# Fetching streamed weights two blocks at a time, with the first blocks of each group kept as one tile

**Chip, cores, metric.** One core of one Trainium2 chip. The metric is the device time of one execution in us; lower is better. Names of engines: PE (TensorE) does the matrix products, DVE (VectorE) and ACT (ScalarE) work on their results, SP (SyncE) issues the transfers of the weights from memory (DMAs).

## The reference

Two layers alternate, each twice, on 2048 tokens of width 640 in bf16: (A) attention over segments of 32 tokens with a recurrent memory of 8 tokens, 32 heads of 192; (B) a small mixer with shifts and two GELUs.

```python
for s in range(n_seg):                        # 64 segments, one after the other
    h = concatenate([mem, x[:, s*32:(s+1)*32]])          # 40 tokens
    q, k, v = h @ Wq, h @ Wk, h @ Wv          # 640 -> 32 x 192 each
    o = softmax(mask(q k^T * scale)) v        # per head
    o = o @ Wo                                # 32 x 192 -> 640
    mem, out[s] = o[:, :8], o[:, 8:]          # the memory feeds the next segment
# mixer: gelu(ln(x) @ w1), shifts, @ w2, residual, gelu(ln @ w3) @ w4, residual
```

The attention weights are 31 MB, of which the kernels below keep some 20 MB on the chip; the recurrence asks for all of them in every segment.

## The kernel before

Attention of both A layers runs together, one layer five segments behind the other, so a step is 80 columns wide. There are 69 steps of 8 head groups; each group has four kinds of weight blocks of 128 rows: k, q and v (5 blocks each) and o (6). The mixer runs in 35 chunks between the steps. A fixed set of blocks stays resident, the rest is streamed in every step, each block by one DMA from the SP queue into a ring. A planner in the kernel simulates all operations with assumed durations, including the DMA, and fixes each engine's order of instructions from that.

```python
RES_BYTES = 154700
RING_A = 10        # slots of one block, attention
RING_B = 5         # slots of one block, mixer
DMA_RATE = 325.0e3 # the planner's assumption, bytes per us
DMA_LAT = 2.2
... # in Plan.place(), for an operation with a DMA:
    srv = max(s + DMA_LAT, srv) + o.dma / DMA_RATE
    done = srv + 0.4
...
    # resident blocks are chosen by a running share: spread evenly among the streamed ones
    for u in rest:
        n = 2 * w_len(u)
        acc += share * n
        if acc >= n / 2 and n <= left:
            res_set.add(u)
            acc -= n
            left -= n
...
def load_unit(t, u, due):                     # u = (kind, group, block)
    ...                                       # resident: load once
    b = Slotted("ra", None)
    b.make = lambda: wring.tile([P, GW], bf16, name="wst", tag=f"ra{b.slot}")
    def fn(op):
        nc.sync.dma_start(out=T(b)[:, 0:n], in_=w_src(u))
    add("SP", 0.06, due, fn, w=(b,), dma=P * n * 2, queue="wa")
    return b, lambda: T(b)
...
# the last product of a step; the o blocks of the last groups may be put off to the step's end
for c in range(GC):
    due = base + STEP - 1 + 0.02 * g if g >= NG - OT_BUFS + 1 else s0 + 2.0 * sl
    wb, wv = load_unit(t, ("o", g, c), ...)
    def f8(op, wv=wv, c=c):
        for m in range(KC):
            nc.tensor.matmul(out=o[:, m, c0:c0 + N], lhsT=w[:, m * P:(m + 1) * P], rhs=o_[:, c, 0:N], ...)
    add("PE", mm_us(N, k=KC), due, f8, r=(wb, B("oT", G % OT_BUFS)), a=(psy,))
```

Of the kernel before, what the change touches and what calls it, by code (L numbers as in the profile page):

```python
# [12 lines left out]
bf16 = mybir.dt.bfloat16  # L13
# [6 lines left out]

LAG = 5
HG = 4
RES_BYTES = 154700
O_RES = 8
RING_A = 10
RING_B = 5
STEP = 48.0
PSUM_BANKS = {"y": 1, "x": 7}
PSUM_USES = {"y": ("y", 1), "P": ("x", 4), "S": ("x", 3), "B": ("x", 2)}
# [205 lines left out]
def kernel(  # L235
# [16 lines left out]
    nc = tc.nc  # L252
    P = 128
    _, S, Dm = A_x.shape
# [5 lines left out]
    KC = Dm // P  # L260
    FC = F // P
    assert (Dm, F, Dh, H, SEG, M) == (640, 1536, 192, 32, 32, 8) and S % (2 * SEG) == 0 and NSEG > 8
    NG = H // HG
    GW = HG * Dh
    GC = GW // P
# [5 lines left out]
    QD = Dm // 4  # L271
# [99 lines left out]
    def B(*key):  # L371
        if key not in bufs:
            bufs[key] = Buf()
        return bufs[key]
# [3 lines left out]
    add = plan.add  # L378
# [9 lines left out]
    def T(b):  # L388
        if b.obj is None:
            b.obj = b.make()  # L390
        return b.obj
# [8 lines left out]
        return ((172 if ps_ else 224) + n) / 1200.0 + 0.02  # L400


    ORDER = []
    for g in range(NG):
        for kind in ("k", "q", "v"):
            ORDER += [(kind, g, kc) for kc in range(KC)]
        if g:
            ORDER += [("o", g - 1, c) for c in range(GC)]
    ORDER += [("o", NG - 1, c) for c in range(GC)]

    def w_len(u):
        return Dm if u[0] == "o" else GW

    res_set = {u for u in ORDER if u[0] == "o" and u[1] >= O_RES}
    left = RES_BYTES - sum(2 * w_len(u) for u in res_set)
    rest = [u for u in ORDER if u not in res_set]
    share = left / sum(2 * w_len(u) for u in rest)
    acc = 0.0
    for u in rest:
        n = 2 * w_len(u)  # L420
        acc += share * n
        if acc >= n / 2 and n <= left:
            res_set.add(u)
            acc -= n
            left -= n

    def w_src(u):
        kind, g, c = u
        if kind == "o":
            return Wo_v[:, g, c, :]  # L430
        return W_v[kind][:, c, GW * g:GW * (g + 1)]

    resident = {}

    def load_unit(t, u, due):
        n = w_len(u)
        if u in res_set:
            if u not in resident:
                tl = wres.tile([P, n], bf16, name="w%s%d_%d" % u)
                b = Buf()  # L440

                def fn(op):
                    nc.sync.dma_start(out=tl[:], in_=w_src(u))
                add("SP", 0.06, due, fn, w=(b,), dma=P * n * 2, queue="wa")
                resident[u] = (b, lambda: tl)
            return resident[u]
        b = Slotted("ra", None)
        b.make = lambda: wring.tile([P, GW], bf16, name="wst", tag=f"ra{b.slot}")

        def fn(op):  # L450
            nc.sync.dma_start(out=T(b)[:, 0:n], in_=w_src(u))
        add("SP", 0.06, due, fn, w=(b,), dma=P * n * 2, queue="wa")
        return b, lambda: T(b)

    def load_b(nm, n, due):

        b = Slotted("rb", None)
        b.make = lambda: wring.tile([P, Dm], bf16, name="wstB", tag=f"rb{b.slot}")
        k = {"w1": n, "w3": KC + n, "w2": KC + FC}.get(nm)
        if nm == "w4":  # L460
            src = w4_v[:, n, :]
        elif nm == "w2" and n < 4:
            src = B_w2[QD * n:QD * n + P, :]
        else:
            src = wbd[k]
        rd = [] if nm == "w4" or (nm == "w2" and n < 4) else [B("wbd", k)]

        def fn(op):
            nc.sync.dma_start(out=T(b)[:], in_=src)
        add("SP", 0.06, due, fn, r=rd, w=(b,), dma=P * Dm * 2, queue="wb")  # L470
        return b, lambda: T(b)

    def order_mixer_weights():

# [35 lines left out]
    def attention_step(t):  # L510
# [12 lines left out]
        def proj_kq(g, s0):  # L523
            G = t * NG + g
            for kind, off in (("k", 0.0), ("q", 0.3 * sl)):
                pq = ps("P", [P, GC, NS], f32, "ps" + kind)
                now = []
                for kc in range(KC):
                    due = s0 + off + kc * 0.05
                    wb, wv = load_unit(t, (kind, g, kc), due)  # L530

                    def fn(op, pq=pq, wv=wv, kc=kc):
                        w, o = wv(), T(pq)
                        for c in range(GC):
                            nc.tensor.matmul(out=o[:, c, 0:N], lhsT=w[:, c * P:(c + 1) * P], rhs=h[:, kc, c0:c0 + N],  # L535
                                             start=pq.begin(), stop=True, skip_group_check=True)
                    now.append(add("PE", mm_us(N, k=GC), due, fn, r=(wb, *hk), a=(pq,), after=last[0]))
                last[0] = now
                if kind == "q":
                    q = qT[G % 2]  # L540

                    def fq(op, pq=pq, q=q):
                        nc.scalar.copy(out=q[:, :, 0:N], in_=T(pq)[:, :, 0:N])  # L543
                    add("ACT", act_us(GC * N), s0 + off, fq, r=(pq,), w=(B("qT", G % 2),))
                else:
                    k_ = kT[G % 2]

                    def fk(op, pq=pq, k_=k_):
                        p4 = T(pq)[:].rearrange("p (h c) n -> p h c n", h=2)
                        k4 = k_[:].rearrange("p (h c) n -> p h c n", h=2)  # L550
                        nc.vector.tensor_copy(out=k4[:, :, 0::3, 0:N], in_=p4[:, :, 0::2, 0:N])  # L551
                    add("DVE", dve_us(4 * N), s0 + off, fk, r=(pq,), w=(B("kT", G % 2, 0),))

                    def fk2(op, pq=pq, k_=k_):
                        p4 = T(pq)[:].rearrange("p (h c) n -> p h c n", h=2)
                        k4 = k_[:].rearrange("p (h c) n -> p h c n", h=2)
                        for hf in range(2):
                            nc.vector.tensor_tensor(out=k4[:, hf, 1:3, 0:N],
                                                    in0=p4[:, hf, 1:2, 0:N].to_broadcast([P, 2, N]),
                                                    in1=halves[:].unsqueeze(2).to_broadcast([P, 2, N]), op=ALU.mult)  # L560
                    add("DVE", 2 * dve_us(2 * N), s0 + off, fk2, r=(pq,), w=(B("kT", G % 2, 1),))

        def proj_v(g, due0):
            G = t * NG + g
            V_, vs = Vt[G % V_BUFS], vTs[G % VT_BUFS]
            vk, Vk = B("vTs", G % VT_BUFS), B("V", G % V_BUFS)
            pv = ps("P", [P, GC, NS], f32, "psv")
            now = []
            for kc in range(KC):
                due = due0 + kc * 0.05  # L570
                wb, wv = load_unit(t, ("v", g, kc), due)

                def fv(op, wv=wv, kc=kc):
                    w, o = wv(), T(pv)
                    for c in range(GC):
                        nc.tensor.matmul(out=o[:, c, 0:N], lhsT=w[:, c * P:(c + 1) * P], rhs=h[:, kc, c0:c0 + N],  # L576
                                         start=pv.begin(), stop=True, skip_group_check=True)
                now.append(add("PE", mm_us(N, k=GC), due, fv, r=(wb, *hk), a=(pv,), after=last[0]))
            last[0] = now

            def fe(op):
                nc.scalar.copy(out=vs[:, :, 0:N], in_=T(pv)[:, :, 0:N])  # L582
            add("ACT", act_us(GC * N), due0, fe, r=(pv,), w=(vk,))
            pt = ps("P", [NS, GC, P], bf16, "psvt")

            def ft(op):
                for c in range(GC):
                    nc.tensor.transpose(out=T(pt)[0:N, c, :], in_=vs[:, c, 0:N], identity=ident[:, :])  # L588
            add("PE", mm_us(P, k=GC), due0 - 2, ft, r=(vk,), w=(pt,))

            def fe2(op):
                nc.scalar.copy(out=V_[0:N, :, 0:Dh], in_=T(pt)[0:N].rearrange("n c f -> n (c f)").rearrange(  # L592
                    "n (i e) -> n i e", i=HG))
            add("ACT", act_us(GW), due0 - 2, fe2, r=(pt,), w=(Vk,))

        def attend(g):
# [65 lines left out]
            add("DVE", dve_us(GC * N), hi - 4, f7, r=(pso,), w=(B("oT", G % OT_BUFS),))  # L662
            for c in range(GC):
                due = base + STEP - 1 + 0.02 * g if g >= NG - OT_BUFS + 1 else s0 + 2.0 * sl
                wb, wv = load_unit(t, ("o", g, c), s0 + (1.9 if g < NG - 1 else 1.2) * sl + 0.03 * c)

                def f8(op, wv=wv, c=c):
                    w, o = wv(), T(psy)
# [163 lines left out]
    def chunk(c):  # L832
# [88 lines left out]
        for i, (a, e) in enumerate(((0, 3), (3, KC))):  # L921
            pz = ps("B", [P, 3, XB], f32, "psh")
            for n in range(a, e):
                due = D(0.15 + 0.04 * n)
                wb, wv = load_b("w1", n, due)

                def fw(op, n=n, a=a, wv=wv, pz=pz):
                    w, o = wv(), T(pz)
# [13 lines left out]
        hs = [ps("B", [XB, HC], f32, "hs") for _ in range(2)]  # L942
        for n in range(5):
            due = D(0.4 + 0.04 * n)
            wb, wv = load_b("w2", n, due)

            def fw(op, n=n, wv=wv):
                w = wv()
# [25 lines left out]
        for i in range(4):  # L974
            a, e = 3 * i, 3 * i + 3
            pz = ps("B", [P, 3, XB], f32, "psh2")
            for n in range(a, e):
                due = D(0.7 + 0.04 * n)
                wb, wv = load_b("w3", n, due)

                def fw(op, n=n, a=a, wv=wv, pz=pz):
                    w, o = wv(), T(pz)
# [6 lines left out]
    def chunk_end(c):  # L989
# [4 lines left out]
        y2 = [ps("B", [XB, HC], f32, "y2") for _ in range(2)]  # L994
        for n in range(FC):
            due = D(1.2 + 0.03 * n)
            wb, wv = load_b("w4", n, due)

            def fw(op, n=n, wv=wv):
                w = wv()  # L1000
# [120 lines left out]
```

## Time and profile before

| | before |
|---|---|
| time | 3761.1 us median (3757.2 to 3765.1, 4 runs) |
| PE busy, DMA engines busy | 92%, 89% |
| DMAs on the SP queue | 5,644 |
| PE's waits for a DMA, 120 to 3640 us, by start spacing | 218 us |

"By start spacing" is my own count and is used throughout: for every group of equal matmuls in the trace I take the time from its start to the next group's start, less the number of matmuls times the usual spacing of their shape (36 ns for 80 columns). The excess is put under whatever the profile names as the end of the wait. It is more than the idle time, which leaves out the pipeline running empty (a matmul of 80 columns lasts 0.20 us in the record, and the next one starts 0.036 us later). The idle time itself is in the view of waits; of the kernel before, 120 to 3640 us (total us, times, longest us):

```profile
PE psk L535 <- DMA wst<-in_A_Wk_dram: 92.5, 92, 2.9
PE psv L576 <- DMA wst<-in_A_Wv_dram: 40.0, 76, 2.1
PE psq L535 <- DMA wst<-in_A_Wq_dram: 39.4, 57, 2.0
PE psk L535 <- ACT hT L695: 19.3, 62, 0.3
PE psy L670 <- DVE oT L661: 16.8, 66, 0.8
```

PE waits mostly for streamed blocks of k, q and v (tile wst).

### The profile page before, as it was taken

The page shows a single profiled execution, that of the slowest core. Times are in us where ns is not written, and L with a number is a line of the kernel's source. Part 1 is how long each engine was busy: PE and PEld are TensorE (multiplying, and loading weights), DVE is VectorE, ACT ScalarE, POOL GpSimd, SP SyncE. Part 2 cuts the span into 40 slices and gives each one's busy share as a digit, 9 for nine tenths or more (in the row PEclk, how much of TensorE's full clock was granted, in tenths as well). Part 3 has the DMA queues.
Part 4 walks back from the last instruction along what each step waited for, and adds up shares of the span by engine and source line. Part 5 has one row for each costly group of instructions (what it writes and reads, how often), then busy time and mean ns, then how long its engine had stood idle before and what let it go on. Part 6 is the DMA issues. An engine that isn't in the chain of part 4 may idle for free.

```text
span 3769.2 us, 193200 instructions
## 1 busy us (share of the span) xinstructions
PE 3457.7 (92%) x84703; PEld 3279.4 (87%) x84703; DVE 2370.4 (63%) x6957; ACT 1727.7 (46%) x3516; POOL 306.8 (8%) x525
## 2 busy tenths in 40 slices
PE   5899999999999999999999999999999999999886
PEld 4788889898999988888999998998999999998774
DVE  1456666666666666666666666666666666666454
ACT  1344444444454544444545454444445444444332
POOL 2000000000000000000000000000000000000000
PEclk9999999999999999999999999999999999999998
DMA  9999898888898988888999988888999988889996
GB/s 316 292 301 284 281 282 272 278 282 281 279 285 271 286 272 268 269 281 277 288 284 283 288 281 276 280 276 278 283 284 288 287 276 280 274 281 288 287 293 190
DMA packets 821967, 1055.33 MB, mean 280 GB/s; under 512 B 95230, under 2 KB 817676, under 8 KB 821120
## 3 DMA queue, kind: packets, MB, share of 16 engines
q1 hardware_dynamic: 812608, 1026.89, 86.2%
q0 software_dynamic: 8512, 16.08, 1.3%
q8 instruction: 662, 10.85, 1.2%
q14 instruction: 185, 1.52, 0.1%
HBM read 1037.35 MB, written 8.19 MB: 277 GB/s over the span
## 4 chain that ended last, share of the span: by engine, by line
PE 66%; DMA 28%; issue 3%; DVE 2%; ACT 1%; SPq 0%; POOL 0%; POOLq 0%; ACTq 0%; DVEq 0%
PE psy L670 13%; PE psk L535 12%; DMA wst<-in_A_Wk_dram 11%; PE psv L576 11%; PE psq L535 10%; DMA wst<-in_A_Wv_dram 7%; DMA wst<-in_A_Wq_dram 5%; PE psvt L588 4%; PE pso L655 3%; PE pss L607 3%; PE y L1002 2%; PE psh L984 2%; PE pst L640 1%; PE hs L952 1%; PE psh L930 1%
## 5 line engine op out<-in xcount | busy, mean ns | idle before, releaser
L535 PEld LDWEIGHTS <-wst 128*128 128x128 bf16 x11592 | 529.2, 100 | 184.0 <-DMA wst<-in_A_Wk_dram 115.5
L661 DVE CAST oT<-pso 128x480 bf16<-128x480 f32 (+1 forms) x552 | 342.3, 620 | 436.6 <-PE pso L655 433.6
L535 PE MATMUL psk<-hT,wk 128*128 128x80 bf16 (+1 forms) x10764 | 590.6, 199 | 26.3 <-ACT hT L695 19.8
L670 PE MATMUL psy<-oT,wo 128*128 128x80 bf16 (+1 forms) x10005 | 574.5, 199 | 23.1 <-DVE oT L661 18.2
L592 ACT COPY V<-psvt 80x768 bf16<-80x768 bf16 (+1 forms) x552 | 438.7, 795 | 339.0 <-PE psvt L588 331.4
L535 PE MATMUL psq<-hT,wq 128*128 128x80 bf16 (+1 forms) x10764 | 554.6, 199 | 7.1 <-DMA wq<-in_A_Wq_dram 4.2
L543 ACT CAST qT<-psq 128x480 bf16<-128x480 f32 (+1 forms) x552 | 292.4, 530 | 557.9 <-PE psq L535 557.3
L576 PE MATMUL psv<-hT,wv 128*128 128x80 bf16 (+1 forms) x9936 | 526.0, 200 | 2.8 <-DMA wv<-in_A_Wv_dram 1.1
L535 PEld LDWEIGHTS <-wk 128*128 128x128 bf16 x10764 | 468.3, 100 | 38.7 <-issue 27.8
L670 PEld LDWEIGHTS <-wo 128*128 128x128 bf16 x10005 | 450.9, 100 | 45.0 <-issue 27.9
L535 PEld LDWEIGHTS <-wq 128*128 128x128 bf16 x10764 | 450.4, 99 | 18.3 <-DMA wq<-in_A_Wq_dram 8.6
L618 DVE CUSTOM_DVE_ANT_1 pss<-pss,mask 80x320 f32<-80x320 f32 x472 | 233.4, 495 | 368.2 <-PE pss L607 367.3
L576 PE MATMUL psv<-hT,wst 128*128 128x80 bf16 (+1 forms) x6624 | 413.3, 200 | 46.4 <-DMA wst<-in_A_Wv_dram 43.7
L535 PE MATMUL psk<-hT,wst 128*128 128x80 bf16 (+1 forms) x5796 | 360.8, 200 | 98.2 <-DMA wst<-in_A_Wk_dram 95.5
L582 ACT CAST vTs<-psv 128x480 bf16<-128x480 f32 (+1 forms) x552 | 292.5, 530 | 330.9 <-PE psv L576 324.7
L670 PE MATMUL psy<-oT,wst 128*128 128x80 bf16 (+1 forms) x6555 | 432.7, 199 | 6.7 <-DMA wst<-in_A_Wo_dram 6.1
L576 PEld LDWEIGHTS <-wv 128*128 128x128 bf16 x9936 | 421.3, 100 | 14.5 <-DMA wv<-in_A_Wv_dram 3.5
L535 PE MATMUL psq<-hT,wst 128*128 128x80 bf16 (+1 forms) x5796 | 360.2, 199 | 45.3 <-DMA wst<-in_A_Wq_dram 43.3
L645 ACT COPY PT<-pst 80x320 bf16<-80x320 bf16 (+1 forms) x552 | 222.1, 402 | 356.9 <-PE pst L640 350.0
L551 DVE CAST kT<-psk 128x320 bf16<-128x320 f32 (+1 forms) x552 | 254.7, 461 | 201.7 <-PE psk L535 200.5
L576 PEld LDWEIGHTS <-wst 128*128 128x128 bf16 x6624 | 307.9, 100 | 70.8 <-DMA wst<-in_A_Wv_dram 62.3
L625 ACT ACTIVATE pss<-pss,sm 80x320 f32<-80x320 f32 (+1 forms) x552 | 258.9, 473 | 136.5 <-DVE sm L618 133.5
(121 smaller groups left out, 5276.2 us busy)
## 6 DMA issues: line engine op xcount, KB each, us to landing
wst<-in_A_Wv_dram SPq DMA_DIRECT2D x1104, 192.0 KB, 4.2
wst<-in_A_Wo_dram SPq DMA_DIRECT2D x1311, 160.0 KB, 4.1
wst<-in_A_Wk_dram SPq DMA_DIRECT2D x966, 192.0 KB, 4.2
wst<-in_A_Wq_dram SPq DMA_DIRECT2D x966, 192.0 KB, 4.2
wstB<-wbd SPq DMA_DIRECT2D x630, 160.0 KB, 4.0
wstB<-in_B_w_dram SPq DMA_DIRECT2D x560, 160.0 KB, 4.1
wk<-in_A_Wk_dram SPq DMA_DIRECT2D x26, 192.0 KB, 4.3
wq<-in_A_Wq_dram SPq DMA_DIRECT2D x26, 192.0 KB, 4.6
```

The lines of the kernel that those rows point to most:

```text
L535: nc.tensor.matmul(out=o[:, c, 0:N], lhsT=w[:, c * P:(c + 1) * P], rhs=h[:, kc, c0:c0 + N], start=pq.begin(), stop=True, skip_group_check= ...
L543: nc.scalar.copy(out=q[:, :, 0:N], in_=T(pq)[:, :, 0:N])
L551: nc.vector.tensor_copy(out=k4[:, :, 0::3, 0:N], in_=p4[:, :, 0::2, 0:N])
L576: nc.tensor.matmul(out=o[:, c, 0:N], lhsT=w[:, c * P:(c + 1) * P], rhs=h[:, kc, c0:c0 + N], start=pv.begin(), stop=True, skip_group_check= ...
L582: nc.scalar.copy(out=vs[:, :, 0:N], in_=T(pv)[:, :, 0:N])
L588: nc.tensor.transpose(out=T(pt)[0:N, c, :], in_=vs[:, c, 0:N], identity=ident[:, :])
L592: nc.scalar.copy(out=V_[0:N, :, 0:Dh], in_=T(pt)[0:N].rearrange("n c f -> n (c f)").rearrange("n (i e) -> n i e", i=HG))
L618: nc.vector.tensor_tensor_reduce(out=o, in0=o, in1=maskt[:].unsqueeze(1).to_broadcast([N, HG, N]), scale=-scale, scalar=3.0e38, op0=ALU.ad ...
L625: nc.scalar.activation(out=o, in_=o, func=ACT.Exp, bias=sm_[0:N, 0:1], scale=-1.0)
L645: nc.scalar.copy(out=Pt[0:N, :, 0:N], in_=T(pst)[0:N, :, 0:N])
L661: nc.vector.tensor_copy(out=o_[:, :, 0:N], in_=T(pso)[:, :, 0:N])
L670: nc.tensor.matmul(out=o[:, m, c0:c0 + N], lhsT=w[:, m * P:(m + 1) * P], rhs=o_[:, c, 0:N], start=psy.begin(), stop=True, skip_group_check ...
```

## The change

The intent: fewer and larger transfers. Of every kind and group the first three blocks (four of o) are resident, as one tile with one load, and the last two are streamed by one DMA into a slot of twice the size. Mixer weights come in pairs too. The planner is told that an issue takes 0.45 us instead of 0.06.

```diff
-RING_A = 10
-RING_B = 5
+RING_A = 5
+RING_B = 3
...
-                add("SP", 0.06, due, fn, w=(b,), dma=P * n * 2, queue="wa")
-                resident[u] = (b, lambda: tl)
...
+    def block(t, kind, g, c, due):
+        n = Dm if kind == "o" else GW
+        cut = (GC if kind == "o" else KC) - 2
+        if c < cut:
+            if (kind, g) not in resident:
+                tl = wres.tile([P, cut, n], bf16, name=f"w{kind}{g}")
...
+                    nc.sync.dma_start(out=tl[:], in_=w_src(kind, g, 0, cut))
...
+        if (t, kind, g) not in streamed:
+            b = Slotted("ra", None)
+            b.make = lambda: wring.tile([P, 2 * GW], bf16, name="wst", tag=f"ra{b.slot}")
+            def fn(op):
+                nc.sync.dma_start(out=T(b)[:, 0:2 * n].rearrange("p (c n) -> p c n", c=2), in_=w_src(kind, g, cut, cut + 2))
+            add("SP", 0.45, due, fn, w=(b,), dma=P * 2 * n * 2, queue="wa")
+            streamed[t, kind, g] = b
+        b = streamed[t, kind, g]
+        return b, lambda: T(b)[:, (c - cut) * n:(c - cut + 1) * n]
...  (load_b: the same for the mixer, slots of [P, 2, Dm])
```

More of the change, by code (lines that the diff above doesn't have):

```diff
@@ L22 @@
 HG = 4
-RES_BYTES = 154700
-O_RES = 8
-RING_A = 10
-RING_B = 5
+RING_A = 5
+RING_B = 3
 STEP = 48.0
@@ L400, in act_us @@
         return ((172 if ps_ else 224) + n) / 1200.0 + 0.02
-    ORDER = []
-    for g in range(NG):
-        for kind in ("k", "q", "v"):
-            ORDER += [(kind, g, kc) for kc in range(KC)]
-        if g:
-            ORDER += [("o", g - 1, c) for c in range(GC)]
-    ORDER += [("o", NG - 1, c) for c in range(GC)]
-    def w_len(u):
-        return Dm if u[0] == "o" else GW
-    res_set = {u for u in ORDER if u[0] == "o" and u[1] >= O_RES}
-    left = RES_BYTES - sum(2 * w_len(u) for u in res_set)
@@ L416, with w_src @@
-    rest = [u for u in ORDER if u not in res_set]
-    share = left / sum(2 * w_len(u) for u in rest)
-    acc = 0.0
-    for u in rest:
-        n = 2 * w_len(u)
-        acc += share * n
-        if acc >= n / 2 and n <= left:
-            res_set.add(u)
-            acc -= n
-            left -= n
-    def w_src(u):
-        kind, g, c = u
+    def w_src(kind, g, a, e):
         if kind == "o":
-            return Wo_v[:, g, c, :]
-        return W_v[kind][:, c, GW * g:GW * (g + 1)]
+            return Wo_v[:, g, a:e, :]
+        return W_v[kind][:, a:e, GW * g:GW * (g + 1)]
@@ L433 @@
     resident = {}
-    def load_unit(t, u, due):
-        n = w_len(u)
-        if u in res_set:
-            if u not in resident:
-                tl = wres.tile([P, n], bf16, name="w%s%d_%d" % u)
+    streamed = {}
+    def block(t, kind, g, c, due):
[4 more added lines that the diff above has]
+                tl = wres.tile([P, cut, n], bf16, name=f"w{kind}{g}")
                 b = Buf()
@@ L442, in fn @@
                 def fn(op):
-                    nc.sync.dma_start(out=tl[:], in_=w_src(u))
-                add("SP", 0.06, due, fn, w=(b,), dma=P * n * 2, queue="wa")
-                resident[u] = (b, lambda: tl)
-            return resident[u]
-        b = Slotted("ra", None)
-        b.make = lambda: wring.tile([P, GW], bf16, name="wst", tag=f"ra{b.slot}")
-        def fn(op):
-            nc.sync.dma_start(out=T(b)[:, 0:n], in_=w_src(u))
-        add("SP", 0.06, due, fn, w=(b,), dma=P * n * 2, queue="wa")
@@ L453, in load_unit @@
-        return b, lambda: T(b)
-    def load_b(nm, n, due):
-        b = Slotted("rb", None)
-        b.make = lambda: wring.tile([P, Dm], bf16, name="wstB", tag=f"rb{b.slot}")
-        k = {"w1": n, "w3": KC + n, "w2": KC + FC}.get(nm)
-        if nm == "w4":
-            src = w4_v[:, n, :]
-        elif nm == "w2" and n < 4:
-            src = B_w2[QD * n:QD * n + P, :]
-        else:
-            src = wbd[k]
-        rd = [] if nm == "w4" or (nm == "w2" and n < 4) else [B("wbd", k)]
-        def fn(op):
-            nc.sync.dma_start(out=T(b)[:], in_=src)
-        add("SP", 0.06, due, fn, r=rd, w=(b,), dma=P * Dm * 2, queue="wb")
-        return b, lambda: T(b)
+                    nc.sync.dma_start(out=tl[:], in_=w_src(kind, g, 0, cut))
@@ new lines, in block @@
+                add("SP", 0.45, due, fn, w=(b,), dma=P * cut * n * 2, queue="wa")
+                resident[kind, g] = b, tl
+            b, tl = resident[kind, g]
+            return b, lambda: tl[:, c, :]
+        if (t, kind, g) not in streamed:
[5 more added lines that the diff above has]
+            streamed[t, kind, g] = b
@@ new lines, in block, with load_b, fn @@
+        b = streamed[t, kind, g]
+        return b, lambda: T(b)[:, (c - cut) * n:(c - cut + 1) * n]
+    mixer = {}
+    def load_b(c, nm, n, due):
+        a = n - n % 2
+        e = min(a + 2, KC if nm in ("w1", "w2") else FC)
+        if (c, nm, a) not in mixer:
+            b = Slotted("rb", None)
+            b.make = lambda: wring.tile([P, 2, Dm], bf16, name="wstB", tag=f"rb{b.slot}")
+            k = {"w1": a, "w3": KC + a, "w2": KC + FC - 4 + a}.get(nm)
+            if nm == "w4":
+                src, rd = w4_v[:, a:e, :], []
+            elif nm == "w2" and a < 4:
+                src, rd = B_w2.rearrange("(g r) d -> r g d", r=QD)[0:P, a:e, :], []
+            else:
+                src = wbd[k:k + e - a].rearrange("b p n -> p b n")
+                rd = [B("wbd", k + i) for i in range(e - a)]
+            def fn(op):
+                nc.sync.dma_start(out=T(b)[:, 0:e - a, :], in_=src)
+            add("SP", 0.45, due, fn, r=rd, w=(b,), dma=P * (e - a) * Dm * 2, queue="wb")
+            mixer[c, nm, a] = b
+        b = mixer[c, nm, a]
+        return b, lambda: T(b)[:, n - a, :]
@@ L529, in proj_kq @@
                     due = s0 + off + kc * 0.05
-                    wb, wv = load_unit(t, (kind, g, kc), due)
+                    wb, wv = block(t, kind, g, kc, due)
                     def fn(op, pq=pq, wv=wv, kc=kc):
@@ L570, in proj_v @@
                 due = due0 + kc * 0.05
-                wb, wv = load_unit(t, ("v", g, kc), due)
+                wb, wv = block(t, "v", g, kc, due)
                 def fv(op, wv=wv, kc=kc):
@@ L664, in attend @@
                 due = base + STEP - 1 + 0.02 * g if g >= NG - OT_BUFS + 1 else s0 + 2.0 * sl
-                wb, wv = load_unit(t, ("o", g, c), s0 + (1.9 if g < NG - 1 else 1.2) * sl + 0.03 * c)
+                wb, wv = block(t, "o", g, c, s0 + (1.9 if g < NG - 1 else 1.2) * sl + 0.03 * c)
                 def f8(op, wv=wv, c=c):
@@ L924, in chunk @@
                 due = D(0.15 + 0.04 * n)
-                wb, wv = load_b("w1", n, due)
+                wb, wv = load_b(c, "w1", n, due)
                 def fw(op, n=n, a=a, wv=wv, pz=pz):
@@ L944, in chunk @@
             due = D(0.4 + 0.04 * n)
-            wb, wv = load_b("w2", n, due)
+            wb, wv = load_b(c, "w2", n, due)
             def fw(op, n=n, wv=wv):
@@ L978, in chunk @@
                 due = D(0.7 + 0.04 * n)
-                wb, wv = load_b("w3", n, due)
+                wb, wv = load_b(c, "w3", n, due)
                 def fw(op, n=n, a=a, wv=wv, pz=pz):
@@ L996, in chunk_end @@
             due = D(1.2 + 0.03 * n)
-            wb, wv = load_b("w4", n, due)
+            wb, wv = load_b(c, "w4", n, due)
             def fw(op, n=n, wv=wv):
```

## The prediction

> **What bounds the kernel now.** I read the page first: engine shares, slices, queues, chain.
>
> ```profile
> PE 3457.7 (92%) x84703; PEld 3279.4 (87%) x84703; DVE 2370.4 (63%) x6957; ACT 1727.7 (46%) x3516; POOL 306.8 (8%) x525
> DMA  9999898888898988888999988888999988889996
> q1 hardware_dynamic: 812608, 1026.89, 86.2%
> PE 66%; DMA 28%; issue 3%; DVE 2%; ACT 1%; SPq 0%; POOL 0%; POOLq 0%; ACTq 0%; DVEq 0%
> ```
>
> TensorE (PE) is busy 92%, the 16 DMA engines 89%; no other engine is near. The chain that ended last is PE work with 28% of DMA in it. So this is a PE kernel that sometimes has no weights. How much that costs is in the busy time by stretch (us, then PE, PEld, DVE, ACT, POOL, clock, DMA share, GB/s) and in the waits of the main stretch:
>
> ```profile
> 0.00:120.00 120.00, 74.20 (x1258) 55.98 (x1258) 22.44 (x94) 20.33 (x50) 26.53 (x51) 1.00 0.95 316
> 120.00:3690.00 3570.00, 3337.90 (x82729) 3189.48 (x82728) 2313.24 (x6768) 1688.69 (x3426) 273.46 (x463) 0.99 0.89 281
> 3690.00:3769.00 79.00, 45.59 (x721) 33.94 (x719) 34.70 (x96) 18.66 (x41) 6.76 (x12) 0.79 0.57 175
> ...
> PE psk L535 <- DMA wst<-in_A_Wk_dram: 93.3, 94, 2.9
> ```
>
> The first 120 us are a load-bound start (resident weights come in), the last 79 us a tail of the mixer with little traffic. I expect both nearly unchanged. In the 3570 us between, PE is idle 232 us. Adding up the PE instructions that followed an idle time by what ended it, 182 us of the 232 are waits for a DMA (242 of them, longest 2.9 us); ACT and DVE make 38 us. Two costs come on top. A restarted stream hides some 0.17 us per wait in "busy" (a matmul lasts 0.20 us in the record, but they follow each other every 0.036 us: 30 of one kind take 1.07 us in the timeline), 242 x 0.17 = 41 us. And the granted clock [...] 0.99 over the stretch is about 33 us. **DMA waits therefore cost about 182 + 41 + 33 = 256 us**, and that is all the change can win.
>
> The question is what makes a weight late. The weights are all issued by one queue, SP. Its issues (duration min/median/max in ns), and four lines of its timeline:
>
> ```profile
> L451 SPq DMA_DIRECT2D wst<-in_A_Wk_dram x966: 327/382/2076, 6.0 to 3695.2; - x194
> L1044 SPq DMA_DIRECT2D xo<-in_A_mem_dram x1: 348/348/348, 5.2 to 5.2; - x1
> ...
> 1559.29 0.85 SPq L451 DMA_DIRECT2D wst<-in_A_Wo_dram  x2
> 1560.24 1.84 SPq L451 DMA_DIRECT2D wst<-in_A_Wk_dram  x2
> 1562.17 0.38 SPq L451 DMA_DIRECT2D wst<-in_A_Wq_dram  x1
> 1562.64 0.86 SPq L451 DMA_DIRECT2D wst<-in_A_Wv_dram  x2
> 1563.59 4.10 SPq L451 DMA_DIRECT2D wst<-in_A_Wo_dram  x3
> ```
>
> One issue takes 0.382 us and the next starts 0.09 us later, so 0.475 us each. 812,608 packets at 144 a DMA (128 rows and 16 more) are 5,643 DMAs: 5,643 x 0.475 = 2,680 us, 71% of the span. I added up the whole SP timeline: besides those 71%, about 700 us (18%) are issues that lasted longer than usual (like the three in 4.10 us above[...]), and about 410 us (11%) are gaps before an issue, the waits for a slot of a ring. **SP is never free**: it issues, is held up, or waits. Then I matched the 211 streamed weight transfers on the chain in order of time with the SP timeline: 189 were issued within 0.15 us of the issue before, 22 after a gap. So a late weight mostly stood in SP's line, and did not wait for a free slot. On the chain such a transfer takes 3.2 to 6.6 us from issue to landing.
>
> [...] 0.475 us against 0.59 us that 192 KB (196.6 thousand bytes) need at the 332 GB/s of 20 to 120 us. [...] the one SP issue with 8 rows took 0.348 us, as long as those with 128, so a fixed part dominates.
>
> **The change part by part.**
> Issues: per attention step, before, 14 k, 14 q, 16 v and 19 o blocks are streamed singly (966, 966, 1104, 1311 over 69 steps): 63 DMAs. After: 8 groups x 4 kinds = 32. A mixer chunk has 34 blocks (5 + 5 + 12 + 12), after 3 + 3 + 6 + 6 = 18 transfers; 35 chunks. Resident tiles: 32 instead of 105. Total after: 69 x 32 + 35 x 18 + 32 + 2 = 2,872 DMAs, half. If the issue stays at 0.475 us, SP issues for 1,364 us, 1,316 us less; it changes from a queue with no slack to one 38% used.
> Bytes: a k, q or v block is 1,536 B a partition, an o block 1,280 B. Resident before: 26 + 26 + 24 = 76 and 29 blocks, 153,856 B; after 8 x (9 x 1,536 + 4 x 1,280) = 151,552 B. Streamed per step before 11.76 MB, after 8 x (6 x 1,536 + 2 x 1,280) x 128 = 12.06 MB: 0.296 MB x 69 = +20.4 MB, +1.9% of 1,055 MB.
> Packets: the rows stay 1,536 or 1,280 B, since the second block of a pair lies elsewhere in the source. Completion packets fall from 90,300 to 46,000; with the added rows some 777,000 packets instead of 812,608 (-4.4%). I can't separate a completion packet's time in the trace; I take bytes and packets together as even for the DMA engines.
> Ring: A has 10 slots of 1,536 B before, 5 of 3,072 B after: the same bytes. B goes from 5 blocks to 6. But a slot is now free only when both its blocks are used, and the first of a pair lands with the second. At 50 us a step, 63 blocks through 10 slots give a slot 7.9 us per turn; 32 pairs through 5 slots give 7.8 us. Of that, before: 0.5 issue + 4.2 landing + about 0.5 use. After I estimate 0.5 + 4.8 (4.2 and one more block at 332 GB/s) + 1.0. The slack falls from 2.7 to 1.5 us. It is a loss, smaller than what SP's line costs now.
> Placement: before, streamed blocks are spread among the resident ones; after, each kind starts with three or four resident blocks (0.6 to 0.7 us of PE) and ends with its pair. Per kind the demand is even, so I count nothing. The kernel's own planner also orders the instructions anew; unknown, no cost.
> Bandwidth check: 281 GB/s x 3,570 us = 1,003 MB, +20 = 1,023 MB; at 332 GB/s this is 3,081 us. If all waits went, the stretch would be about 3,310 us and the DMA engines 93% used. That is too close to be free of waits.
> Sum: 256 us of DMA waits; I keep 40% for bandwidth bursts and the coarser ring, so 60%, 154 us, goes: 3,761 - 154 = 3,607; I add 8 us for the larger first resident transfers and the added bytes in the load-bound start. **Predicted: 3,615 us.**
>
> **Rivals.**
> 1. The DMA engines are the real limit and SP's line only mirrors it. For: the 700 us of prolonged issues, and a DMA share of 0.8 to 1.1 in the stretches where PE waited (at 1560 to 1565.5 us). Against: those windows moved only 234 to 332 GB/s, while 332 is held for 100 us at the start. Then time stays or rises with the bytes: 3,720 to 3,790 us.
> 2. Five coarse slots become the bound: SP waits for slots, PE for pairs. For: slack of only 1.5 us. Against: only 22 of 211 critical transfers waited for a slot. Would give 3,750 to 3,900 us.
> 3. The issue of a pair costs twice as much [...]: SP stays at 70%, and the gain shrinks to what fewer completions give: 3,680 to 3,760 us. Against: 8 rows cost as much as 128.
> 4. All goes well and only the start, the tail and ACT and DVE waits remain: 3,500 us.
>
> **Range and chances.** The mechanism gives 3,540 to 3,680 us and I hold it for likely, 0.7. Rivals 1 and 3 together get 0.22, nearly all within 2% (3,687 to 3,838). Rival 2 gets 0.08. The range 3,500 to 3,730 leaves about one in ten on each side.
>
> **What would show it.** Right: SP issues halved to about 2,870 and each near 0.4 us; hardware queue packets near 777,000; PE's waits for DMA in the main stretch below 110 us; clock above 0.99; GB/s near 299; DMA's part of the chain under 20%. Wrong: a median issue near 0.75 us (rival 3); GB/s unchanged with a DMA share above 0.9 and long issues growing (rival 1); SP's waits for PE growing and landing over 6 us (rival 2). The prediction fails if pairs land so late that PE waits as often as now, or if the new order of instructions makes waits elsewhere.

## More of the kernel before

The end of a step is a chain in which each operation needs the one before: scores, softmax, `pst` (transpose), PT (ACT), `pso` (PE), oT (DVE), `psy` (PE), then ACT writes the memory columns of hT, and the first product `psk` of the next step needs them. Other PE work, put in between, can hide it.

## The result

3720.6 us median (3715.4 to 3722.1, 4 runs) against 3761.1 us. The ratio is 0.989 (95%: 0.9873 to 0.9907). A ratio here is the mean time of one kernel's runs over that of the other's of the same rounds, so not quite the ratio of the medians. That is a gain of 1.1%, within 2%: clear of noise, but 41 us where I forecast 146.

The page of the kernel after, two of the lines that answer to those of before (PE is busy 92%, as it was):

```profile
q1 hardware_dynamic: 776960, 1046.77, 87.4%
PE 74%; DMA 16%; DVE 4%; issue 4%; ACT 1%; SPq 0%; POOL 0%; DVEq 0%; ACTq 0%; POOLq 0%
```

The packets are as worked out (776,960; 45,944 of them are small ones of 4 B, 16 a DMA), DMA's part of the chain fell from 28% to 16%; and DVE (2% to 4%) and "issue" (3% to 4%) rose. The start stayed at 120 us and the tail at some 80; the main stretch now ends at 3640:

```profile
120.00:3640.00 3520.00, 3308.12 (x82514) 3181.59 (x82510) 2307.30 (x6749) 1675.72 (x3416) 272.28 (x462) 0.99 0.90 290
```

PE's idle time in the main stretch is 3520.0 - 3308.1 = 212 us, hardly less than the 232 of before. The granted clock stayed too: worked out to one more digit from the clock records, 0.991 in both main stretches. SP, in contrast, changed altogether: issues, and a piece of its timeline (start us, length us):

```profile
L430 SPq DMA_DIRECT2D wst<-in_A_Wk_dram x552: 367/368/2024, 6.0 to 3642.0; - x184
...
1500.44 0.37 SPq L430 DMA_DIRECT2D wst<-in_A_Wv_dram  x1
1502.71 0.37 SPq L430 DMA_DIRECT2D wst<-in_A_Wk_dram  x1
```

A pair is issued in 0.37 us, no longer than a single block. Between issues SP stands idle, mostly waiting for a slot: added up from the single records, some 2,190 us beyond the usual gap, where it was 640; what issues took beyond the usual fell from 520 to 210 us. Of the 100 streamed transfers that are on the chain now, 91 were issued after a gap; before, 41 of 199. So the line of issues is gone. (The prediction has other figures for before because it read merged rows of the timeline, which hide the gaps between issues of one kind: of its "4.10" for three issues, 2.60 us are two gaps.) The waits of the kernel after, 120 to 3640 us:

```profile
PE psy L658 <- DVE oT L649: 63.6, 93, 1.4
PE psk L523 <- ACT hT L683: 40.1, 67, 1.0
...
PE psq L523 <- DMA wst<-in_A_Wq_dram: 22.0, 32, 1.9
...
PE psk L523 <- DMA wst<-in_A_Wk_dram: 16.6, 35, 1.8
...
PE psv L564 <- DMA wst<-in_A_Wv_dram: 13.0, 25, 1.0
PE psv L564 <- issue: 12.8, 15, 2.2
```

The waits for weights shrank to a third. In their place, the two waits at the end of a step went from 36 to 104 us, and a new kind, "issue", appeared. By start spacing, 120 to 3640 us:

| PE waited for | before | after | difference |
|---|---|---|---|
| DMA | 218 | 67 | -151 |
| DVE | 30 | 86 | +57 |
| ACT | 30 | 54 | +24 |
| "issue" (nothing the profile shows) | 3 | 53 | +50 |

**The end of a step** explains DVE and ACT. PE, DVE and ACT there, before:

```profile
1757.39 0.34 PE L670 MATMUL psy<-oT,wo 128*128 128x80 bf16 x5 [0.23 <-DVE oT L661]
1757.57 0.34 PE L670 MATMUL psy<-oT,wst 128*128 128x80 bf16 x5
1757.75 0.45 PE L655 MATMUL pso<-PT,V 80*128 80x80 bf16 x8
1758.04 0.53 PE L670 MATMUL psy<-oT,wo 128*128 128x80 bf16 x10
1758.24 0.66 DVE L661 CAST oT<-pso 128x480 bf16<-128x480 f32 x1 [0.90 <-PE pso L655]
...
1760.50 0.38 PE L535 MATMUL psk<-hT,wk 128*128 128x80 bf16 x6 [0.31 <-ACT hT L695]
```

and after:

```profile
1710.42 0.88 PE L658 MATMUL psy<-oT,wo 128*128 128x80 bf16 x20 [0.26 <-DVE oT L649]
1711.13 0.53 PE L658 MATMUL psy<-oT,wst 128*128 128x80 bf16 x10
1711.49 0.46 PE L643 MATMUL pso<-PT,V 80*128 80x80 bf16 x8
1711.98 0.66 DVE L649 CAST oT<-pso 128x480 bf16<-128x480 f32 x1 [1.61 <-PE pso L643]
1712.69 0.88 PE L658 MATMUL psy<-oT,wo 128*128 128x80 bf16 x20 [0.75 <-DVE oT L649]
```

In both, oT of the last group takes DVE 0.66 us. Before, the last `pso` (1757.75) was ordered ahead of most of the previous group's 30 `psy` matmuls, and these ran while DVE worked. After, all 30 come first (1710.42, 1711.13), then `pso`, and PE has nothing left: it stands for 0.75 us. In nearly every second step it is 1.07 us, and PE then waits 0.98 us for ACT instead of 0.31. The planner's schedules say the same: built again for a check, PE's gaps before `psy` are 73 us in all in the plan of before, and 108 us in that of after. The planner even gives the total: its schedule ends at 3,511 us for before and at 3,577 us for after. It needs no chip, so this could have been read before the run.

**The "issue" waits** fall in the middle of blocks whose weights and inputs are there. PE of the kernel after:

```profile
1959.04 0.50 PE L564 MATMUL psv<-hT,wst 128*128 128x80 bf16 x9
1961.73 0.28 PE L564 MATMUL psv<-hT,wst 128*128 128x80 bf16 x3 [2.19 <-issue]
```

The 12 matmuls of one pair stop after nine: the second block, in use for three matmuls already, can't be what is missing. The page of both kernels lists a queue of the kind "instruction" (q8): 662 packets and 10.85 MB, 16.4 KB a packet. PE's 169,406 instructions (84,703 matmuls and as many weight loads) and some 200 semaphore instructions between them, divided by 662, are 256 a packet, so I take this queue to be PE's. I numbered all of PE's instructions in order and took the number modulo 256 where PE stopped: all 60 "issue" waits of the whole kernel lie at one place (193 or 194), while the 112 waits for streamed weights lie spread over all places. And each of the 60 waits ended 1.2 to 1.6 us after a packet of this queue had landed, where packets are 5.6 us apart on average. So I read these waits as PE waiting for its own instructions. The page counts the packets of this queue among those of the 16 DMA engines, with 1.2% of the 16 engines' span; those of SP's queue have 87.4% in after.

### The profile page after: what moved, and what is told of

Same layout as the page of the kernel before. It is cut to its first block, busy times and chain, and to the rows that moved or that the text cites. A ratio compares the mean times of both kernels' runs of the same rounds, so it can differ in the third digit from the quotient of the medians.

```text
span 3720.4 us, 187465 instructions
## 1 busy us (share of the span) xinstructions
PE 3424.1 (92%) x84703; PEld 3275.8 (88%) x84703; DVE 2368.1 (64%) x6957; ACT 1718.8 (46%) x3516; POOL 305.8 (8%) x525
## 3 DMA queue, kind: packets, MB, share of 16 engines
q1 hardware_dynamic: 776960, 1046.77, 87.4%
q8 instruction: 662, 10.85, 1.2%
## 4 chain that ended last, share of the span: by engine, by line
PE 74%; DMA 16%; DVE 4%; issue 4%; ACT 1%; SPq 0%; POOL 0%; DVEq 0%; ACTq 0%; POOLq 0%
PE psy L658 14%; PE psv L564 13%; PE psk L523 13%; PE psq L523 12%; DMA wst<-in_A_Wq_dram 6%; DMA wst<-in_A_Wk_dram 5%; PE psvt L576 4%; DMA wst<-in_A_Wv_dram 4%; PE pss L595 4%; PE pso L643 3%; PE y L990 3%; PE pst L628 2%; DVE oT L649 2%; PE psh L972 2%; PE psh L918 1%
## 5 line engine op out<-in xcount | busy, mean ns | idle before, releaser
L658 PE MATMUL psy<-oT,wo 128*128 128x80 bf16 (+1 forms) x11040 | 521.4, 199 | 75.9 <-DVE oT L649 63.6
L523 PE MATMUL psk<-hT,wk 128*128 128x80 bf16 (+1 forms) x9936 | 477.0, 200 | 49.1 <-ACT hT L683 40.4
L564 PE MATMUL psv<-hT,wv 128*128 128x80 bf16 (+1 forms) x9936 | 454.7, 199 | 10.7 <-issue 7.9
L523 PE MATMUL psq<-hT,wq 128*128 128x80 bf16 (+1 forms) x9936 | 451.3, 200 | 12.4 <-DMA wq<-in_A_Wq_dram 9.2
L523 PEld LDWEIGHTS <-wk 128*128 128x128 bf16 x9936 | 407.5, 100 | 59.5 <-issue 54.5
L523 PEld LDWEIGHTS <-wq 128*128 128x128 bf16 x9936 | 398.7, 100 | 24.3 <-DMA wq<-in_A_Wq_dram 10.0
L564 PEld LDWEIGHTS <-wv 128*128 128x128 bf16 x9936 | 395.0, 100 | 27.0 <-issue 8.9
L564 PE MATMUL psv<-hT,wst 128*128 128x80 bf16 (+1 forms) x6624 | 344.2, 199 | 21.5 <-DMA wst<-in_A_Wv_dram 15.9
L523 PE MATMUL psq<-hT,wst 128*128 128x80 bf16 (+1 forms) x6624 | 330.3, 199 | 30.0 <-DMA wst<-in_A_Wq_dram 25.8
L618 DVE TENSOR_REDUCE sm<-pss 80x4 f32<-80x320 f32 (+1 forms) x552 | 251.4, 455 | 79.1 <-ACT pss L613 78.5
```

What stands on the lines that cost most here:

```text
L523: nc.tensor.matmul(out=o[:, c, 0:N], lhsT=w[:, c * P:(c + 1) * P], rhs=h[:, kc, c0:c0 + N], start=pq.begin(), stop=True, skip_group_check= ...
L564: nc.tensor.matmul(out=o[:, c, 0:N], lhsT=w[:, c * P:(c + 1) * P], rhs=h[:, kc, c0:c0 + N], start=pv.begin(), stop=True, skip_group_check= ...
L618: nc.vector.reduce_sum(out=sm_[0:N, 4:4 + HG], in_=o, axis=AX.X)
```

## The experiments

Kernels of one call ran on one chip, with the kernel before beside them. On those chips before took 3776 to 3782 us, so compare ratios. All experiments that edit `fn` leave the planner's input alone; I compared the planned orders, and they are the same operation by operation (the matmuls of the traces too).

| run | ratio to before (95%) | waits by start spacing: DMA, DVE, ACT, "issue" |
|---|---|---|
| before | 1 | 218, 30, 30, 3 |
| after | 0.9890 (0.9873 to 0.9907) | 67, 86, 54, 53 |
| f1 after, again | 0.9858 (0.9829 to 0.9886) | 73, 87, 57, 48 |
| e1 pairs split | 1.0056 (1.0021 to 1.0090) | 151, 80, 53, 1 |
| e7 a tiny DMA more per pair | 1.0113 (1.0086 to 1.0139) | 203, 80, 54, 8 |
| e5 mixer pairs split | 0.9817 (0.9791 to 0.9843) | 77, 83, 56, 32 |
| e8 before, resident blocks as after | 0.9994 (0.9969 to 1.0019) | 187, 51, 33, 6 |
| e6 before, planner's rate 400 | 1.0039 (1.0011 to 1.0067) | 244, 26, 31, 4 |
| e4 after, planner's rate 400 | 0.9764 (0.9728 to 0.9801) | 111, 40, 32, 52 |
| f2 e4 and e5 | 0.9745 (0.9726 to 0.9764) | 126, 41, 32, 47 |
| f3 f2, planner's PE delay 0.15 | 0.9882 (0.9863 to 0.9901) | 172, 24, 33, 38 |
| e2, e3 without streamed weights | 0.9396, 0.9172 | see below |

### Was it the line of issues? (e1, e7, e5)

e1 fetches each pair with two issues:

```diff
-nc.sync.dma_start(out=T(b)[:, 0:2*n].rearrange("p (c n) -> p c n", c=2), in_=w_src(kind, g, cut, cut + 2))
+for i in range(2):
+    nc.sync.dma_start(out=T(b)[:, i*n:(i+1)*n], in_=w_src(kind, g, cut + i, cut + i + 1)[:, 0, :])
```

(and so for the mixer).

> The kernel after, with each pair fetched by two issues of one block each into the same slot: slots, placement, bytes and the order of all other instructions stay; only the number of SP issues goes back to some 5,600. Theory (SP's line of issues made weights late): PE's waits for DMA in the main stretch rise from 66 us (by start spacing) to 170 to 230 us, the time to 3,800 to 3,880 us. Rival (the waits fell because of where the resident blocks lie, or through the ring): time stays within 15 us of 3,721, DMA waits stay under 90 us.

Measured: 3793.8 us, ratio 1.0056; waits for DMA 151 us instead of 67. The direction is the theory's, the size a little under its range (170 us, 3,800 us). The rival allowed 15 us; against after (0.9858 to 0.9890) the step is 1.7 to 2.0%, some 62 to 75 us. That is what coalescing is worth in this order. Of the 200 streamed transfers that PE waited for in e1, SP issued 141 without a wait just before (187 of 230 in the kernel before); 46 came after SP had waited for an earlier transfer to land, 13 after a wait for a slot.

e7 leaves the pairs whole and only makes the line longer:

```diff
+dum = [const.tile([8, 8], bf16, name=f"dum{i}") for i in range(16)]
+def dummy():
+    nc.sync.dma_start(out=dum[ndum[0] % 16][:], in_=A_mem0[0][:, 0:8]); ndum[0] += 1
 ...
     nc.sync.dma_start(... the pair ...)
+    dummy()
```

> The kernel after with one tiny extra DMA (8 rows of 16 bytes, into scratch) issued after every weight pair: the pairs stay pairs, SP's issues go back to some 5,700, bytes stay. Theory (the line of issues, not the size of a transfer): DMA waits go up to 130 to 200 us and time to 3,770 to 3,830 us, as in e1. Rival (single transfers as such, with their later landing, made e1 slower): within 20 us of 3,721. The mid-block waits (52 us in after, 1 in e1): if they come with the large transfers they stay near 50; if they come with a queue that runs far ahead, they go to a few us.

Measured: 3822.4 us, ratio 1.0113, waits for DMA 203 us. The 2,838 tiny transfers of 128 B move 0.36 MB in the whole kernel, and each holds SP for 0.37 us. Of the kernel e7, 120 to 3640 us:

```profile
PE psk L531 <- DMA wst<-in_A_Wk_dram: 81.6, 98, 3.0
PE psy L666 <- DVE oT L657: 63.1, 92, 1.4
```

The waits for the k blocks are back near their 92.5 us, with the transfers as large as in after. So more transfers made weights late here (203 us of waits against 67) with no weight transfer smaller: the rival (single transfers as such) predicted no change. But e7 does not show that the issue time alone does it. In the trace of after SP's transfers use eight completion semaphores in turn (each of the 2,864 from the ninth on has that of the transfer eight before it; 5,636 of 5,636 in before), and SP waits for the landing of that earlier transfer: of the 2,506 for which the trace gives it, and of 4,931 in before, none was issued ahead of it (the closest came 0.015 us after). If e7's take turns in the same way, the tiny transfers have half of the eight places, which leaves half as many weights under way: an estimate. SP's waits for a DMA, 120 to 3640 us, added up, are 202 us in after, 191 in e1 and 477 in e7; one line of after and one of e7:

```profile
SPq L430 <- DMA wst<-in_A_Wv_dram: 60.7, 68, 2.1
SPq L436 <- DMA wst<-in_A_Wv_dram: 113.6, 206, 2.4
```

Of the 215 streamed transfers that PE waited for in e7, 115 were issued after such a wait, 71 without a wait just before, 29 after a wait for a slot. e1, by the same estimate, has half the bytes under way of after, since its transfers are half as large (192 KB against 384). The end of the step costs the same as in after, since the order is the same. And the "issue" waits fell to 8 us with the same large transfers: they were 53 us in after, where SP ran ahead with them, and 1 us in e1.

e5 splits only the mixer's pairs (the second edit of e1).

> The kernel after with only the mixer's pairs fetched block by block (560 issues more, 3,430 in all); order, slots and placement as after. Theory (SP's line matters when it is full): SP is 43% issuing instead of 37%, so nearly nothing changes, time 3,715 to 3,745 us. If each single transfer costs on its own (a share of e1's 73 us by number of issues, 560 of 2,768), about +15 us.

Measured: 3712.3 us, ratio 0.9817. It is just below the theory's range (3,715 us). As the theory has it, 560 issues more showed no cost here; "issue" waits were 32 us. It may be slightly faster than after (0.9858 to 0.9890), but the two were not timed on one chip.

### Order, or waits that had been hidden? (e2, e3)

Both kernels without the streamed attention weights, wrong results on purpose, orders unchanged:

```diff
-    nc.sync.dma_start(out=..., in_=w_src(...))      # the streamed block or pair
+    return
 ...
-return b, lambda: T(b)[...]
+return b, lambda: (the first resident block of k)
```

> Wrong result on purpose: the kernel after, with the streamed attention weights not fetched (a resident block is used in their place); the order of all instructions as in the kernel after. It shows what that order costs when weights are never late. Theory (the new order brings the waits for DVE and ACT at the end of each step): those waits stay near 139 us (DVE 85, ACT 54), DMA waits nearly vanish, time 3,560 to 3,620. If the waits in mid-block that the profile calls issue (52 us) come from instruction fetches standing behind the weights, they vanish too; if they are something of PE, they stay.

> Wrong result on purpose: the kernel before, treated in the same way, in the order of before. Theory (order): waits for DVE and ACT stay near the 58 us of the kernel before, and the time is 60 to 90 us below that of e2. Rival (these waits were always there, hidden while PE waited for weights): they rise to 120 to 140 us and the time is within 15 us of e2.

Measured: 3545.6 us in the order of after, 3460.7 us in that of before. With weights never late, the order of before is 85 us faster; by start spacing, DVE and ACT waits between 120 and 3400 us are 136 us in e2 and 63 in e3, 73 us of the 85. Waits of e2 and of e3, 120 to 3400 us:

```profile
PE psy L658 <- DVE oT L649: 62.6, 91, 1.4
PE psk L523 <- ACT hT L683: 39.5, 65, 1.0
```

```profile
PE psk L535 <- ACT hT L695: 19.6, 63, 0.3
PE psy L670 <- DVE oT L661: 17.5, 67, 0.8
```

They are the same as in after and before, to a us or so. The rival (these waits had been hidden behind late weights) is out: e3 has no late weights to speak of and shows no more of them. They belong to the order that the planner made. "Issue" waits: 0.3 us in e2, against 53 in after, so they come with the traffic of the weights. e2 was faster than I expected (3,560 to 3,620).

### What makes the planner's order, and does it help to change it? (e8, e4, e6)

e8 is the kernel before with after's choice of resident blocks, still single:

```diff
-    res_set = ... (spread by a running share)
+    res_set = {u for u in ORDER if u[2] < (GC if u[0] == "o" else KC) - 2}
```

> The kernel before with only the choice of resident blocks of after (first three or four of each kind; 2% more bytes), everything singly in the rings of before. Tells what the placement costs by itself: e1 was 33 us slower than before with as many issues. If the placement (and its bytes, and the order that the planner makes of it) is the cause, 3,780 to 3,800 us; if it is the coarse slots and the order they bring, 3,755 to 3,770 us.

Measured: ratio 0.9994, the time of before; by the absolute times I had given, 3777.5 us fell between my two cases, because before took 3778.5 us on that chip. Judged against that, placement and 2% more bytes cost nothing in time. Its DVE waits are 51 us, between the 30 of before and the 86 of after: part of the worse order comes with the placement, the rest with pairs in coarse slots. The planner's schedules, built again, end at 3,511 us (before), 3,542 (e8) and 3,577 (after). As I read it, the planner's model of the DMA (325 thousand bytes per us, pairs that land together) makes weights late on paper, and it fills the gaps with the `psy` blocks that the end of the step would have needed; e4 tests the rate. The altered issue cost (0.06 to 0.45) has next to no part: planned with 0.06, 96 of 15,200 PE operations stand elsewhere.

e4 gives the planner of after a faster DMA; transfers and slots stay:

```diff
-DMA_RATE = 325.0e3
+DMA_RATE = 400.0e3
```

> The kernel after, with only the planner's assumed DMA rate set from 325 to 400 thousand bytes per us: the same transfers and slots, another order of instructions. Theory (order): waits for DVE and ACT fall from 139 to 70 to 100 us, time 3,650 to 3,695. Rival (the DMA engines bound, so that any order that waits less at the step's end waits for weights instead): DMA waits rise by as much, time 3,705 to 3,735.

Measured: 3684.7 us, ratio 0.9764. Waits at the step's end, 120 to 3640 us:

```profile
PE psy L658 <- DVE oT L649: 25.3, 63, 0.6
PE psk L523 <- ACT hT L683: 20.4, 66, 0.3
```

Both are near those of before again; DVE and ACT together fell, by start spacing, from 140 to 73 us. But waits for DMA grew from 67 to 111 us: 44 of the 67 us came back there. The rival was partly right: where PE waited less at the step's end, it waited more for weights. Whether the DMA engines stop it (their share is 0.91 at 293 GB/s between 120 and 3400 us) or the ring (120 of the 132 streamed transfers that PE waited for were issued right after a wait for a slot) no run separates.

e6 makes the same edit to the kernel before.

> The kernel before with only the planner's assumed DMA rate set to 400. Theory (before, weights late by SP's line are the limit, the order is secondary): DVE and ACT waits stay near 58 us, DMA waits near 218 us, time within 25 us of before. If the rate by itself brings e4's gain, time falls by 36 us or more and the change has no part in it.

Measured: ratio 1.0039. DMA waits went from 218 to 244 us, and nothing was won: the rate by itself brings no gain. The end of the step had little to win here (DVE 30 to 26 us), so e6 does not tell what a better order would be worth while SP's line stands.

### A version meant to beat both (f1, f2, f3)

> The kernel after, unchanged, beside the next two on one chip, since the kernel before took 3,761 us on the first chip and 3,776 to 3,779 us on those of the experiments. Expected ratio to before 0.985 to 0.991.

f1 measured 3726.5 us, ratio 0.9858, with the same split of waits as after. The gain of after is 1.1 to 1.4%, from chip to chip.

f2 is e4 with e5's single mixer transfers.

> A version meant to beat both: pairs for attention, single transfers for the mixer (e5), the planner's rate at 400 (e4). If the two gains add (order: 81 us of waits at the step's end halved; mixer singly: 20 us less of mid-block waits), ratio 0.968 to 0.975. If the DMA engines bind, as e4's grown DMA waits hint, no better than e4: 0.974 to 0.98.

f2 measured 3684.5 us, ratio 0.9745 against f1's 0.9858 on the same chip. It beats both kernels. It lies in both of the ranges that I had given, and it can't be told from e4 (their intervals overlap), so a gain of the mixer's single transfers on top of e4 is not shown.

f3 also changes `PE_LAT = 0.25` to `0.15` in the planner.

> f2 with the planner's assumed delay from PE to another engine cut from 0.25 to 0.15 us. If the planner was too careful and kept fillers away from the step's end, DVE and ACT waits fall below 60 us and the ratio is 0.96 to 0.97; if 0.25 is right, its order is wrong on the chip and the waits for DVE and ACT in mid-step grow: ratio above 0.98.

f3 measured 3737.0 us, ratio 0.9882. DVE waits fell to 24 us, and DMA waits rose to 172. My either-or was too narrow: the end of the step got better and mid-step waits for DVE and ACT did not grow; the loss went to weights. Why this order makes them so late I did not follow up.

## Why the prediction was wrong

**What held.** Weights were late because of the number of transfers in SP's queue: with the order, slots and bytes of after, splitting the pairs (e1) raised the waits for DMA from 67 to 151 us. How much of this is issue time, as the prediction has it, and how much the wait for an earlier transfer to land (SP's waits for a DMA: 202 us in after, 477 in e7), which it did not see, stays open; in before, 187 of the 230 late weights came without a wait of SP just before, 29 after a wait for a landing. The issue time did not grow with a second block (0.37 us after 0.38), the issues halved, the packets were 776,960. Rival 3 is out. The term "60% of 256 us, 154 us" was met by the waits for DMA, which fell by 151 us, but partly by luck: 33 of the 256 us were put down to the clock, and the clock did not change (0.991 in both), so the waits fell by more than 60% of theirs. Of the signs of being right nearly all came true (only GB/s stayed lower, 290); they watched the weights alone, and the time did not follow.

**What failed** is the sentence "The kernel's own planner also orders the instructions anew; unknown, no cost." It should have been a cost: +57 us of waits for DVE and +24 us for ACT, 81 us, nearly all at the ends of steps. e2 against e3 isolates it (85 us), e4 takes most of it away again. The prediction's last sentence had named such waits as a way to fail, but its sum gave them nothing. The code excerpt held the warning: the planner simulates the DMA, so changing transfers changes the order of everything.

**What I had not thought of**: the "issue" waits, in my reading PE's own instructions arriving late, +50 us. -151 + 57 + 24 + 50 = -20 us; the excess that goes under no wait fell by another 10 us or so, and the measured -41 us is of that size, no more: the stretch of 120 to 3640 us holds a little more of the work of after than of before.

A smaller error lies in the 151 itself. It is not all coalescing: with after's order and the issues split again (e1), DMA waits are 151 us, not 218. As I read it, PE standing elsewhere (DVE 80 us, ACT 53 in e1) gives late weights time to land, so these waits are no sum of independent parts. Coalescing by itself takes away 84 us of them (e1).

**The other rivals.** Rival 2 (coarse slots): SP does wait for slots now, some 2,000 us, and 88 of the 92 streamed transfers that PE still waited for were issued right after such a wait, so the ring bounds what is left, 67 us at most; e1 at ratio 1.0056 and e8 at 0.9994 put slots and the order they bring at about 0.6% together. Rival 1 (the DMA engines) is not shown to limit after; in e4, 44 us came back as waits for DMA, through the engines or through the ring.

**Open.** Why the "issue" waits come (pairs 53 us, the same pairs with a tiny DMA between 8, singles 1) I can show only by their conditions. After PE has passed the place where those waits lie (193 or 194), the next packet of the instruction queue starts, in the median, 1.8 us later in after, 1.3 us in e1 and e7, and 0.4 us in e2, without the attention weights. What holds it no run shows. Nor does one separate the issue time from the wait for the transfer eight before: that would take pairs with more issue time and nothing more in flight.

## What to carry to other kernels

Look at the issuing queue as an engine of its own: 5,644 issues of 0.475 us filled 71% of the span, and most transfers that held up PE (187 of 230) were issued without a wait just before. Ask too how many transfers can be under way: in before none of 4,931 was issued ahead of the landing of the one eight before it, so eight of 384 KB can hold twice the bytes of eight of 192 KB (an estimate). When a kernel's order is made by a planner that models the transfers, a change to transfers is also a change to the order: compare the planned end and the waits at the recurrence before and after, and fit the planner's rate again (here 325 to 400 was worth 0.9 to 1.3% in the kernel after, and nothing in the kernel before). A wait taken away is a gain only until the next one in the same place, so count what is left when it is gone; running the kernel without the traffic (e3) shows that floor.
